# Last attention round projected in native float32, the outputs' last additions moved to VectorE, the small feed-forward group last

## The chip, the cores and the metric

The kernel runs on one core of a Trainium2 chip. The metric is the device time in microseconds of one launch, the median of several runs. A profile is one more execution, with every engine's instructions on record. Engines are named as the profile does: PE is TensorE (PEld its weight loads), DVE VectorE, ACT ScalarE, POOL GpSimd, SP SyncE; a trailing q is an engine's sequencer.

## The reference

A gated mix of two branches over one input x of 2048 tokens by 512 features:

```python
x = A_x                                    # [1, 2048, 512]
g = sigmoid((x * gate_w).sum(-1, keepdims=True))
# A: 32 heads of 16, one shared key and value head
q = (x @ wq).reshape(B, S, 32, 16).transpose(0, 2, 1, 3)
p = softmax(einsum("bhqd,bkd->bhqk", q, x @ wk) * 16 ** -0.5)
a = einsum("bhqk,bkd->bhqd", p, x @ wv).transpose(0, 2, 1, 3).reshape(B, S, 512) @ wo
# B: feed-forward, 512 -> 1792 -> 512
b = silu(x @ w1) @ w2
out = g * a + (1 - g) * b
```

All arrays are float32.

## The kernel before

Large products are made of float16 halves: each operand is split into a float16 value and a float16 rest, and three products (high by high, high by rest, rest by high) make one float32-like product. Attention's second product works otherwise: the exponentials stand in float32, and a key step of 64 keys takes either the route "A" and "B" (bfloat16 upper part, then the rest that VectorE subtracts out at L1158) or the route "N", one native float32 product, which needs no VectorE work.

Queries are cut into NCH = 4 chunks of 512 tokens, heads into NO = 4 groups of 8. That makes 16 rounds, and each round goes over 32 key steps of two half steps: 1024 score tiles (L1146) and 1024 exponentials on ScalarE (L1152, 128 by 1024 each). Into this loop the feed-forward is woven: for each chunk, F = 14 tiles of 128 in groups GF = (4, 4, 4, 2), first h (`ffn_h`, tanh on ScalarE, SiLU and a cast of the high half over a GpSimd DMA, L884), then four output products per group (`ffn_o`, one for each block of 128 tokens). When a chunk's four attention rounds are normalised, its projection by wo runs too (`out_proj`). Every output block of 128 tokens is summed in an accumulator `acc` on VectorE (`add_out`, L819 and L821), with the gate as a per-token scale, and stored when its last part is in; the last chunk has one part more, since its fourth round is projected by itself.

The order inside the loop is written by a small planner when the program is built: it keeps a clock for PE, ACT and DVE with fixed costs (PASS 0.217, WHOLE 0.866, EXP 0.905 and so on), and at each step takes the engine whose next task starts first. For PE the candidates are a score tile "S", a PV product "P", and a stream "F" of feed-forward and projection passes. A pass of the stream joins one tile that uses the array's lower 64 rows with one that uses its upper 64 rows; if there is no partner, half the array stays empty. The stream's sequence comes from `outs()`, which goes through `blocks`, the list of chunks and groups; the last chunk has an order of its own, `LAST`. VectorE's work stands in `tasks` with due times. The loop ends when at most four feed-forward outputs are left.

Behind the loop (L1418 to L1452) the stream's rest is finished, the last round is normalised (`norm_a` to `norm_b`: transposes, a sum, a reciprocal, a product, a transpose), O is split into halves (`norm_c`, L124 and L125), and the last round is projected by twelve float16 products of 128 by 512 (L844). A flag `aside` is on there: a part that is added while it is on goes over ScalarE (a scaled copy into `e`, L816) and GpSimd (an addition, L817), and its block is stored from ScalarE's queue; the last three blocks are added by VectorE and stored from SyncE's queue.

After this every engine loads a flag (L1456), jumps over a second pass that does not run for these inputs (L1457), waits for its queues, and meets the others at the end (L1482). The flag comes from `chores`, which gather maxima in the last quarter of the loop; they use `qx`, the query buffer, as scratch.

Of the kernel before, what the change touches and what calls it, by code (L numbers as in the profile page):

```python
# [21 lines left out]
NF = max(GF)  # L22
LAST = (3, 0, 1, 2)
ACCS = 4
# [24 lines left out]
def kernel(  # L49
# [62 lines left out]
    for o in range(NO):  # L112
        for c in range(NCH):
            qd[o, c] = dram.tile([128, 2, 512], F16, name=f"qd{o}_{c}")
            sh[o, c] = dram.tile([8, 2, 512], F16, name=f"sh{o}_{c}")
    md = dram.tile([128], F32, name="md")

    def split(a1, a2, a, scale):
# [95 lines left out]
    def cleared():  # L214
        for q in qb_:
            nc.gpsimd.memset(q, 0.0)
        for t_ in (VP, VF, nus):
# [478 lines left out]
    def chores():  # L696
# [13 lines left out]

        qf = qx.bitcast(F32)

        def gather():

            mt, mr, mq = qf[:, 384:416], qf[:, 416:417], qf[:, 448:480]
# [4 lines left out]
            nc.vector.transpose(mq, qf[:, 416:448])  # L720
            nc.sync.dma_start(md.rearrange("(a b) -> a b", a=4), mq[0:128:32])

        m, m1 = qf[0:1, 0:128], qf[0:1, 128:160]

        def row():
            nc.sync.dma_start(m, md.rearrange("(o p) -> o p", o=1))

        g = qf[0:1, 256:256 + 4 * len(RANGES)].rearrange("p (a b) -> p a b", a=4)

# [65 lines left out]
    def attention(ctx, scale_of, t_scale, shifts, split_pieces, chores, q_todo, bounds, early, gates_):  # L795
# [10 lines left out]

        def add_out(c, t, po, gate):
            n = c * 4 + t
            if n not in accs:
                assert n < ACCS or parts[n - ACCS] == n_parts(n - ACCS)  # L810
                accs[n] = wp.tile([128, D], F32, name="acc", bufs=ACCS)
            a = accs[n]
            if aside[0]:
                assert n in parts
                e = wp.tile([128, 512], F32, name="e", bufs=2)
                nc.scalar.activation(e, po, AF.Copy, scale=gate[:, n:n + 1])  # L816
                nc.gpsimd.tensor_tensor(a, a, e, op=OP.add)  # L817
            elif n not in parts:
                nc.vector.tensor_scalar(a, po, gate[:, n:n + 1], None, op0=OP.mult)  # L819
            else:  # L820
                nc.vector.scalar_tensor_tensor(a, po, gate[:, n:n + 1], a, op0=OP.mult, op1=OP.add)  # L821
            parts[n] = parts.get(n, 0) + 1
            if parts[n] == n_parts(n):
                (nc.scalar if aside[0] else nc.sync).dma_start(out[n * 128:n * 128 + 128], a)

# [145 lines left out]
        def bound(new, t):  # L971
# [6 lines left out]
            def shift(t):  # L978
# [5 lines left out]
                def close(t):  # L984
                    note()
                    open_q.pop()
                    if not kept:
                        e_left[0] += 1

                task(t + 9, t, 0.6, close)  # L990

            task(t, t, 0.6, shift, True)

        urgent = []
# [115 lines left out]

        def norm_c(st, key, t):
            O = wp.tile([128, 2, 512], F16, name="O", bufs=NO)
            split_v(O[:, 0], O[:, 1], st["OT"])
# [4 lines left out]

            if o == NO - 1 or c == NCH - 1 and o == NO - 2:
                all_ = {q: Os.pop((c, q)) for q in range(NO) if (c, q) in Os}  # L1120
# [196 lines left out]
        def pe_next():  # L1317
# [8 lines left out]
            if x:  # L1326
                r, s = x
                cands.append((r, 1 if n_exp[0] - 2 * s >= LAG else 3 if left_of[s][0] != "N" else 4, "P", s))
            if n_early[0]:
# [52 lines left out]
        def on_act(t, x):  # L1382
# [4 lines left out]
            exponential(p)  # L1387
            exp_done[p] = t + EXP_DONE
            n_exp[0] += 1
            decide(*divmod(p, 2))  # L1390
# [19 lines left out]
        pack_next(pack(), 0.0)  # L1410
        piece_next(0.0)
        if gates_:
            task(20.0, 0.0, 0.6, lambda t: gates_())
# [72 lines left out]
```

## Time and profile before

| | us |
|---|---|
| three runs | 1048.05, 1048.07, 1049.81 |
| median | 1048.07 |
| profiled execution | 1049.44 |
| its span, first to last instruction | 1047.6 |
| TensorE busy in the span | 1013.8 |
| ScalarE busy | 998.4 |
| VectorE busy | 940.8 |
| GpSimd busy | 60.4 |

The span is shorter than the execution's own time by what lies around the instructions. Busy times are sums over stages with different limits. A matmul's end in the profile is modelled, so TensorE's share says little of its peak.

### The profile page before, as it was taken

To read this page: it belongs to the slowest core of one execution; us is meant where nothing else is said; L and a number is where in the kernel's file an instruction comes from. 1 tells how busy PE (TensorE), PEld (TensorE's weight loads), DVE (VectorE), ACT (ScalarE), POOL (GpSimd) and SP (SyncE) were. 2 spreads that over 40 slices of the span, in tenths; PEclk is the share of its full clock that TensorE was granted. 3 is DMA by queue.
4 is the path that set the end of the run, shared out by engine and by line. 5 is a ranking of instruction groups with operands and counts; after the bars stand their busy time and mean duration, and the time that the engine had idled before them with its cause. 6 is when DMAs were issued, how large, how long until landed. Compare 5 with 4: busy or idle time off the path is not lost.

```text
span 1047.6 us, 63988 instructions
## 1 busy us (share of the span) xinstructions
PE 1013.8 (97%) x30021; PEld 555.7 (53%) x30021; DVE 940.8 (90%) x1196; ACT 998.4 (95%) x1119; POOL 60.4 (6%) x134
## 2 busy tenths in 40 slices
PE   9989999999999999999999999999999999999994
PEld 6345555555555555555555555555555555555562
DVE  6888887799999999999989999998999999999994
ACT  5899999999999999999999999999999999999991
POOL 3011111100000000000000000000000000000001
PEclk9999999999999999999999999999999999999998
DMA  6222222211011020111001021010110110101001
GB/s 215 87 64 69 80 64 69 65 44 24 5 31 37 24 45 14 35 23 21 19 14 34 34 49 19 20 29 9 40 24 9 46 33 14 34 9 19 9 4 45
DMA packets 28699, 40.18 MB, mean 38 GB/s; under 512 B 5897, under 2 KB 19978, under 8 KB 28426
## 3 DMA queue, kind: packets, MB, share of 16 engines
q0 software_dynamic: 10656, 15.73, 7.3%
q1 hardware_dynamic: 17194, 19.94, 6.1%
q8 instruction: 237, 3.88, 1.5%
q10 hardware_dynamic: 576, 0.33, 0.1%
q14 instruction: 36, 0.29, 0.1%
HBM read 20.11 MB, written 8.52 MB: 27 GB/s over the span
## 4 chain that ended last, share of the span: by engine, by line
PE 56%; ACT 28%; issue 7%; DVE 6%; DMA 1%; SPq 0%; ACTq 0%; DVEq 0%; POOLq 0%
ACT P L1152 26%; PE pm L840 22%; PE pv L1172 18%; PE S L1146 14%; DVE L L1158 2%; ACT e L871 2%; DVE raw L1158 1%; DMA xn<-in_A_x_dram 1%; PE pm L844 1%; PE pk L448 1%; DVE e L874 1%; DVE acc L821 0%; PE pt L328 0%; DVE mxs L139 0%; DMA H<-e 0%
## 5 line engine op out<-in xcount | busy, mean ns | idle before, releaser
L1152 ACT ACTIVATE P<-S 128x1024 f32<-128x1024 f32 x1024 | 959.2, 1077 | 13.5 <-PE pv L1172 7.4
L1146 PE MATMUL S<-qb,KT 50*32 50x512 f16 x8192 | 445.8, 380 | 14.7 <-ACT P L1152 11.8
L1158 DVE TENSOR_TENSOR L<-P 128x1024 f16<-128x1024 f32 x332 | 394.9, 1217 | 30.3 <-ACT P L1152 29.6
L1146 PEld LDWEIGHTS <-KT 50*32 50x32 f16 x8192 | 202.4, 89 | 265.0 <-issue 176.8
L840 PE MATMUL pm<-xs,w1s 64*32 64x512 f16 x5376 | 303.4, 375 | 2.1 <-DVE acc L821 0.9
L840 PE MATMUL pm<-w2s,H 64*32 64x512 f16 x5376 | 297.2, 375 | 0.9 <-DVE e L874 0.5
L1172 PE MATMUL pv<-P,VF 64*32 64x512 f32 x4096 | 277.1, 589 | 0.0
L1158 DVE TENSOR_TENSOR raw<-P 128x1024 f16<-128x1024 f32 x180 | 215.3, 1217 | 7.6 <-ACT P L1152 7.2
L840 PEld LDWEIGHTS <-w1s 64*32 64x32 f16 x5376 | 128.3, 92 | 54.3 <-issue 11.8
L840 PEld LDWEIGHTS <-H 64*32 64x32 f16 x5376 | 126.9, 92 | 53.1 <-issue 11.4
L1172 PE MATMUL pv<-P,VP 64*32 64x512 bf16 x2048 | 116.9, 386 | 0.0
L1172 PEld LDWEIGHTS <-VP 64*32 64x32 f16 x4096 | 74.5, 92 | 37.0 <-issue 9.9
L1172 PEld LDWEIGHTS pv<-P,VF 64*32 64x32 f32 x4096 | 80.9, 106 | 23.5 <-issue 2.9
L1172 PE MATMUL pv<-L,VP 64*32 64x512 f16 x1328 | 91.5, 376 | 0.1
L840 PE MATMUL pm<-xs,wqs 64*32 64x512 f16 x1152 | 84.8, 375 | 0.0
L884 POOL DMA_DIRECT2D H<-e x56 | 29.7, 531 | 767.0 <-DVE e L874 710.9
L840 PE MATMUL pm<-wo_s,O 64*32 64x512 f16 x1440 | 70.8, 375 | 0.1
L1172 PE MATMUL pv<-raw,VP 64*32 64x512 f16 x720 | 56.4, 376 | 0.0
L874 DVE SCALAR_TENSOR_TENSOR e<-e,pm 128x512 f32<-128x512 f32 x56 | 38.3, 684 | 11.4 <-ACT e L871 11.2
L888 DVE TENSOR_TENSOR H<-e,H 128x512 f16<-128x512 f32 x56 | 38.3, 684 | 3.5 <-DMA H<-e 3.5
L821 DVE SCALAR_TENSOR_TENSOR acc<-pm,g,acc 128x512 f32<-128x512 f32 x46 | 34.4, 749 | 7.7 <-PE pm L840 6.8
L840 PEld LDWEIGHTS <-wqs 64*32 64x32 f16 x1152 | 34.8, 92 | 11.5 <-issue 2.2
(179 smaller groups left out, 477.4 us busy)
## 6 DMA issues: line engine op xcount, KB each, us to landing
H<-e POOLq DMA_DIRECT2D x56, 128.0 KB, 2.3
qb<-qd SPq DMA_DIRECT2D x192, 32.0 KB
raw<-in_B_w_dram POOLq DMA_DIRECT2D x24, 256.0 KB, 3.1
xn<-in_A_x_dram SPq DMA_DIRECT2D x8, 512.0 KB
out_dram<-acc SPq DMA_DIRECT2D x15, 256.0 KB
qd<-qx SPq DMA_DIRECT2D x12, 256.0 KB
raw<-in_A_wo_dram POOLq DMA_DIRECT2D x4, 256.0 KB, 2.9
qb<-sh SPq DMA_DIRECT2D x60, 2.0 KB
```

What stands on the lines that cost most here:

```text
L448: nc.tensor.matmul(pk[64 * h:64 * h + 64], wkvs[:, i, kt], xs[:, j, kt, (c + h) * 512:(c + h) * 512 + 512], start=kt + n == 0, stop=kt == ...
L821: nc.vector.scalar_tensor_tensor(a, po, gate[:, n:n + 1], a, op0=OP.mult, op1=OP.add)
L840: nc.tensor.matmul(self.bank[32 * m:32 * m + 32], l(i, rows, 32 * m), r(j, rows), start=first, stop=last)
L844: nc.tensor.matmul(self.bank, l(i, slice(0, 128), 0, 128), r(j, slice(0, 128)), start=first, stop=last)
L871: nc.scalar.activation(e, o.bank, AF.Tanh, scale=t_scale)
L874: nc.vector.scalar_tensor_tensor(e, e, 1.0, o.bank, op0=OP.add, op1=OP.mult)
L884: nc.gpsimd.dma_start(H[:, 0], e)
L888: nc.vector.tensor_tensor(H[:, 1], e, H[:, 0], op=OP.subtract)
L1146: nc.tensor.matmul(sc[32 * m:32 * m + 32, f], KT[b:b + 50, k0:k0 + 32], qtile[i][b:b + 50, m // 2, j], start=True, stop=True)
L1152: nc.scalar.activation(probs[s][:, 2 * j:2 * j + 2], banks.pop(p), AF.Exp, scale=scale_of(*rounds[steps[s][0]]))
L1158: nc.vector.tensor_tensor(lows[s, j], probs[s][:, js], upper(probs[s])[:, js], op=OP.subtract)
L1172: nc.tensor.matmul(pvs[i][h][32 * j:32 * j + 32], a[r], b[r], start=k == 0 and n != "B", stop=k == NK - 1 and n != "A")
```

## The change

Five edits, all in or behind the loop of attention:

- `LAST` goes from (3, 0, 1, 2) to (0, 1, 2, 3): the group of two feed-forward tiles is the last one of the last chunk.
- The last round is not split into halves (`norm_c` returns at once). Instead the transposed O (`state["OT"]`, float32) is the stationary operand of four native float32 products with the last 128 rows of wo, which `load_last` brings as float32 into `qx` once no query block is open any more. `qx` is no longer free as scratch, so the chores use the new tile `sc` and the first row of `ident`. The gate of these products is `g2`, the gate with the scale of wo multiplied in, made once, 60 exponentials before the end.
- `add_out` loses its way over ScalarE and GpSimd: all additions are VectorE's. Behind the loop the odd blocks are stored from ScalarE's queue and the even ones from SyncE's.
- When the last exponential is planned, a PV product goes ahead of the stream (priority 1).
- Behind the loop the normalisation goes ahead of the additions that are left; then come the four products, each into a bank of its own, and their additions.

```diff
-LAST = (3, 0, 1, 2)
+LAST = (0, 1, 2, 3)
...
+    sc = consts.tile([128, 96], F32)
+    g2 = consts.tile([128, 4], F32)
...
-        def add_out(c, t, po, gate):
+        def add_out(c, t, po, gate, m=None):
             n = c * 4 + t
+            m = n if m is None else m
...
-            if aside[0]:
-                assert n in parts
-                e = wp.tile([128, 512], F32, name="e", bufs=2)
-                nc.scalar.activation(e, po, AF.Copy, scale=gate[:, n:n + 1])
-                nc.gpsimd.tensor_tensor(a, a, e, op=OP.add)
-            elif n not in parts:
-                nc.vector.tensor_scalar(a, po, gate[:, n:n + 1], None, op0=OP.mult)
+            if n not in parts:
+                nc.vector.tensor_scalar(a, po, gate[:, m:m + 1], None, op0=OP.mult)
             else:
-                nc.vector.scalar_tensor_tensor(a, po, gate[:, n:n + 1], a, op0=OP.mult, op1=OP.add)
+                nc.vector.scalar_tensor_tensor(a, po, gate[:, m:m + 1], a, op0=OP.mult, op1=OP.add)
             parts[n] = parts.get(n, 0) + 1
             if parts[n] == n_parts(n):
-                (nc.scalar if aside[0] else nc.sync).dma_start(out[n * 128:n * 128 + 128], a)
+                (nc.scalar if aside[0] and t % 2 else nc.sync).dma_start(out[n * 128:n * 128 + 128], a)
...
                     open_q.pop()
+                    if not open_q:
+                        load_last()
...
+        wl = qx.bitcast(F32)
+
+        def load_last():
+            nc.sync.dma_start(wl, wo[(NO - 1) * 128:NO * 128])
...
         def norm_c(st, key, t):
+            if key == rounds[-1]:
+                return
...
-            if o == NO - 1 or c == NCH - 1 and o == NO - 2:
+            if o == NO - 1 - (c == NCH - 1):
...
-                cands.append((r, 1 if n_exp[0] - 2 * s >= LAG else 3 if left_of[s][0] != "N" else 4, "P", s))
+                cands.append((r, 1 if n_exp[0] - 2 * s >= LAG or n_exp[0] == 2 * len(steps) else 3 if left_of[s][0] != "N" else 4, "P", s))
...
+            if p == 2 * len(steps) - 60:
+                task(t + 20, t, 0.1, lambda t: nc.vector.tensor_scalar(g2, gg[:, 4 * (NCH - 1):4 * NCH], split_pieces.so, None, op0=OP.mult))
...
-        ends, banks_ = [], halves()
+        ends, banks_ = [], halves() + halves()
         while work.next or left[0]:
             o, work.next = work.next or next(seq), None
             if o is not None:
-                o.bank = banks_.pop(0) if banks_ else bank()
+                o.bank = banks_.pop(0)
                 whole([o], range(len(o.mm)))
                 ends.append(o)
         while tasks:
-            n = min((n for n, x in enumerate(tasks) if x[1]() is not None), key=lambda n: tasks[n][0])
+            n = min((n for n, x in enumerate(tasks) if x[1]() is not None), key=lambda n: (tasks[n][4], tasks[n][0]))
             now["DVE"] += on_dve(now["DVE"], n)
-        for o in ends[:1]:
+        for o in ends:
             o.add()
-        outs_ = [o() for o in urgent]
-        for o, b in zip(outs_, [bank(), bank()] + halves()):
-            o.bank = b
-        whole(outs_, range(2))
-        whole(outs_, range(2, 3 * NO))
-        for o in ends[1:] + outs_:
-            o.add()
-            aside[0] = o in ends
-
+        banks_ += [bank() for _ in ends]
+        for t, b in enumerate(banks_):
+            nc.tensor.matmul(b, state["OT"][:, t * 128:t * 128 + 128], wl, start=True, stop=True)
+        for t, b in enumerate(banks_):
+            add_out(NCH - 1, t, b, g2, t)
```

More of the change, by code (lines that the diff above doesn't have):

```diff
@@ L216, in cleared @@
             nc.gpsimd.memset(q, 0.0)
-        for t_ in (VP, VF, nus):
+        for t_ in (VP, VF, nus, sc):
             nc.gpsimd.memset(t_, 0.0)
@@ L709, in chores @@
         todo.append(lambda: absmax(mxs[:, M_VV:M_VV + 1], VF[:, :, 1:17], AX.XY))
-        qf = qx.bitcast(F32)
         def gather():
-            mt, mr, mq = qf[:, 384:416], qf[:, 416:417], qf[:, 448:480]
+            mt, mr, mq = sc[:, 0:32], sc[:, 32:33], sc[:, 64:96]
             nc.vector.tensor_reduce(mr[0:64], um, axis=AX.X, op=OP.min)
@@ L719, in gather @@
             nc.vector.tensor_reduce(mr, mt, axis=AX.X, op=OP.max)
-            nc.vector.transpose(mq, qf[:, 416:448])
+            nc.vector.transpose(mq, sc[:, 32:64])
             nc.sync.dma_start(md.rearrange("(a b) -> a b", a=4), mq[0:128:32])
-        m, m1 = qf[0:1, 0:128], qf[0:1, 128:160]
+        m, m1 = ident[0:1], sc[0:1, 0:32]
         def row():
             nc.sync.dma_start(m, md.rearrange("(o p) -> o p", o=1))
-        g = qf[0:1, 256:256 + 4 * len(RANGES)].rearrange("p (a b) -> p a b", a=4)
+        g = ident[0:1, 0:4 * len(RANGES)].rearrange("p (a b) -> p a b", a=4)
         def check(n0):
@@ L1411, in attention @@
         piece_next(0.0)
+        if not open_q:
+            load_last()
         if gates_:
```

## The prediction

> **What bounds the kernel now.** I read the page first, then the instructions of the program's last lines (the branch at L1457 and the closing at L1482), then the chain of waits from 1000 us on, then windows and tiles of the stretch that the change rewrites.
>
> ```profile
> span 1047.6 us, 63988 instructions
> PE 1013.8 (97%) x30021; PEld 555.7 (53%) x30021; DVE 940.8 (90%) x1196; ACT 998.4 (95%) x1119; POOL 60.4 (6%) x134
> ...
> 530.00:776.00 246.00, 244.03 (x7656) 134.80 (x7635) 230.38 (x259) 243.85 (x272) 7.40 (x14) 1.00 0.12 27
> 776.00:1022.50 246.50, 240.79 (x7432) 135.59 (x7423) 229.34 (x280) 244.76 (x272) 7.93 (x15) 1.00 0.10 21
> ```
>
> The first two lines are the page's, the last two are windows (length, then busy time of PE, PEld, DVE, ACT and POOL). The second window is the last quarter of the loop, and it is the only part of the loop that the change re-plans. ScalarE is busy 244.76 of 246.50 us there. So before the last score the new order can win at most 1.74 us of ScalarE's idle time, however much TensorE saves.
>
> Behind the loop the bound is another. These are the sequencers' instructions at the end (count, minimum/median/maximum ns, first and last start in us):
>
> ```profile
> L1457 POOLq INC_SWDGE_SEM  x1: 1991/1991/1991, 1037.3 to 1037.3; - x1
> L1457 ACTq COMPARE_BRANCH  x1: 54/54/54, 1037.9 to 1037.9; - x1
> L1457 SPq COMPARE_BRANCH  x1: 45/45/45, 1038.4 to 1038.4; - x1
> L1457 SPq EVENT_SEMAPHORE  x8: 17/17/17, 1041.7 to 1042.2; - x8
> L1482 POOLq DRAIN  x3: 50/107/7414, 1039.3 to 1047.3; - x3
> L1482 SPq DRAIN  x3: 7/7/7, 1043.0 to 1047.0; - x3
> L1482 ACTq DRAIN  x2: 8/8/8, 1041.0 to 1047.0; - x2
> L1482 DVEq DRAIN  x2: 10/14/17, 1039.6 to 1047.0; - x2
> L1482 PEldq DRAIN  x2: 8/10/13, 1039.0 to 1047.1; - x2
> ```
>
> SyncE, ScalarE, VectorE and TensorE reach their first closing drain at about 1043.1, 1041.0, 1039.6 and 1039.0. GpSimd starts a drain at 1039.3 that lasts 7.41 us, to 1046.75; only then do the others go on, at 1047.0. So the last 3.65 us before the final 0.84 us belong to GpSimd alone. Its drain is late because of what stands ahead of it:
>
> ```profile
> 990.83 0.53 POOL L884 DMA_DIRECT2D H<-e  x1 [28.76 <-DVE e L874]
> 1029.53 1.28 POOL L817 TENSOR_TENSOR acc<-acc,e 128x512 f32<-128x512 f32 x1 [38.18 <-ACT e L816]
> 1032.41 1.28 POOL L817 TENSOR_TENSOR acc<-acc,e 128x512 f32<-128x512 f32 x1 [1.60 <-ACT e L816]
> 1035.61 1.26 POOL L817 TENSOR_TENSOR acc<-acc,e 128x512 f32<-128x512 f32 x1 [1.91 <-ACT e L816]
> ```
>
> The timeline of POOL: its loop work ends at 990.83, and the three additions of L817 hold it until 1036.87. The chain of waits does not show this, because it ends at the last arithmetic:
>
> ```profile
> 1002.92 0.86 PE pv L1172 x16
> ...
> 1022.64 0.22 PE S L1146 x8
> ...
> 1023.08 0.86 PE pm L840 x32
> ...
> 1026.11 0.98 PE pv L1172 x16
> 1027.09 1.31 DVE T L1089 x2
> ...
> 1031.39 0.72 DVE T L1109
> ...
> 1032.14 0.44 DVE O L124
> ...
> 1032.63 0.61 PE pm L844 x2
> ...
> 1035.00 0.76 DVE acc L821
> ...
> 1036.32 0.74 DVE acc L821
> ```
>
> **The change part by part.** Edits with one answer first. The additions of L816/L817 disappear from ScalarE and GpSimd and go to VectorE. The new load of wo's last 128 rows in float32 (256 KB) stands on SyncE's queue at about score 769 of 1024; it holds the queue as long as a store of the same size (0.36 us, SPq row below), and what is queued behind it is the exchange of the maxima and the query loads of the next round, 64 exponentials ahead of their use: nothing. Nor do the scratch tiles, the small product for the gates and one memset at the start cost anything that the end waits for.
>
> Loop. Counted in the built instruction order, the passes between score 769 and the last score are 440 feed-forward or projection passes instead of 443, with two drains of TensorE fewer, the rest alike. The row "0.86 x32" is four passes of eight, 0.215 each: 0.65 us less TensorE work, of which ScalarE's bound lets little through. I take 0.2, bounds 1.7 of gain (all of the idle time above) and 1.7 of loss (the idle time doubled).
>
> From the last score to the last PV product. Before: 1022.86 to 1027.09, 4.23 us. After, the order puts PV first and holds one half product, two passes and three native float32 products (0.86 each, row at 1002.92): 0.22 + 0.43 + 2.58 = 3.23, a gain of 1.0. Together the last PV ends at 1027.09 - 1.2 = 1025.9.
>
> Normalisation is unchanged: 1027.09 to 1032.11 is 5.02 us, so the transposed O is there at 1030.9. The two halves of O (L124/L125, 0.5 us ahead of the first product) fall away.
>
> Projection. Four native products of 128 columns by 512 take the place of twelve float16 ones. Nearest row: 0.86 us for one native pass of the whole array, so 3.46. The price could be more by exposed weight loads, but the products are long; I take 3.46. Their signals come in pairs in the built program (after the second and the fourth product), so two additions start after each. Meanwhile VectorE does the two left-over feed-forward additions:
>
> ```profile
> L821 DVE SCALAR_TENSOR_TENSOR acc<-pm,g,acc x46: 739/750/754, 208.2 to 1024.0; 128x512 f32<-128x512 f32 x46
> L821 DVE SCALAR_TENSOR_TENSOR acc<-S,gg,acc x2: 742/742/742, 1035.7 to 1036.3; 128x512 f32<-128x512 f32 x2
> L824 SPq DMA_DIRECT2D out_dram<-acc x15: 332/356/1187, 329.4 to 1037.7; - x15
> L824 ACTq DMA_DIRECT2D out_dram<-acc x1: 363/363/363, 1036.9 to 1036.9; - x1
> ```
>
> Two at 0.75 are 1.5 us, inside the 1.73 of the first two products. If those ran late, each would move the end by up to 0.75.
>
> Clock. This is the cost that is not shown. TensorE's feed-forward rest behind the last PV was long before and is short after:
>
> ```profile
> 1026.77 4.83 PE L840 MATMUL pm<-w2s,H 64*32 64x512 f16 x112
> ...
> 1035.00:1035.50 0.50, 0.39 (x2) 0.00 (x0) 0.50 (x1) 0.50 (x1) 0.00 (x0) 1.00 0.00 0
> 1037.50:1038.00 0.50, 0.00 (x0) 0.00 (x0) 0.00 (x0) 0.00 (x0) 0.00 (x0) 0.92 0.51 160
> 1038.00:1038.50 0.50, 0.00 (x0) 0.00 (x0) 0.00 (x0) 0.00 (x0) 0.00 (x0) 0.50 1.05 369
> ```
>
> Before, TensorE worked until 1031.60 and started again at 1032.63: 1.03 us idle, and the clock stayed. After, eight passes and a drain (1.9 us) stand behind the last PV instead of twenty, so TensorE idles from 1027.8 to 1030.95, 3.15 us. The windows show what an idle time can do: the last product ended at 1035.39, and the granted clock (the 0.92) fell to half at 1037.92, 2.5 us later. A gap of 3.15 us is nearer to the 2.5 that had the fall than to the 1.03 that had none. So I let the clock fall. No row shows how long it stays low: the bounds are no extra time and 3.46 us (all four products at half clock); I take the middle, 1.6.
>
> The Trainium skill, "TensorE: Matmul & The Clock Gate", section "What's actually happening", says that the clock halves after at least one idle window of about 3.4 us, free-running, and comes back after a busy one; the trace agrees that the clock halves, but its fall came 2.5 us after the last product, within less than a full idle window. By the page's window a low stretch would cost about 1.7 us.
>
> End. The products end at 1030.95 + 3.46 + 1.6 + 0.17 (pipeline) = 1036.2; the third addition ends at 1036.9, the fourth at 1037.6. SyncE stores blocks 0 and 2, ScalarE blocks 1 and 3. From the issue of its last store SyncE needed 5.39 us to its drain before (1037.7 to 1043.1: issue, branch, 3.3 us to the first instruction behind it, checks), so it drains at 1042.35. ScalarE needed 4.1 from issue to drain (1036.9 to 1041.0): 1041.7. GpSimd's wait, INC_SWDGE_SEM and drain (0.4 + 2.0 + 7.4 = 9.9 us with gaps, from 1036.87 to 1046.75) now follow its last H cast. In the built order that stands 36 VectorE instructions ahead of the end, 16 of them of this kind:
>
> ```profile
> L1158 DVE TENSOR_TENSOR L<-P 128x1024 f16<-128x1024 f32 x332 | 394.9, 1217 | 30.3 <-ACT P L1152 29.6
> ```
>
> At 1.22 us for these and 0.75 for most others that is over 30 us, so the loop hides them. Without that cover they would cost up to 3.65 us again. The barrier's rest adds 0.84: 1043.2 us against 1047.6, 4.4 us less. The profiled execution took 1049.44 us, its span and 1.84 around it, 1.37 above the median of the three runs; I take the difference off the median: 1048.07 - 4.4 = 1043.7.
>
> **The rivals.**
> (B) The clock holds. The gap is 3.15 us and the only fall seen came after an idle time that never ended; for it speaks that 1.03 us did nothing. By the skill's page named above this is the likelier course, since a 3.15 us gap cannot fill a 3.4 us window. Then the 1.6 go: 1042.1.
>
> (C) GpSimd's 7.41 us drain is not its own length but waits for the others' quiet. Against it: it started before the last stores had landed and outlasted SyncE by 3.65 us, with no wait named. For it: the trace has it once only, at the very end. Then it would end as far behind the last addition as now: 1046.75 - 1037.06 = 9.7 us behind 1037.6, which is 1048.1 in the span with the 0.84; on the median 1048.6 at the low clock, and 1047.0 at the full one.
>
> (D) The re-planned last quarter starves ScalarE. With the small group last, outputs and casts fall at other places, and each exponential that waits for its scores is paid in full, since ScalarE is the bound. Price: 256 exponentials by 0.027 us each are 6.9 us. It decides from 4.4 + 2.1 = 6.5 us of added idle time on, against 1.74 now; the quarter before lost 2.15, so nothing in the trace has that size. Then 1043.7 + 6.9 = 1050.6.
>
> That the change does not do what it says I rule out: the four native products stand in the built order, and no addition on GpSimd.
>
> **How the numbers follow.** My forecast has 0.62, B 0.20, C 0.12, D 0.06. The forecast alone spans 1041.8 (a low stretch of little cost, a better loop) to 1046.0 (all products at half clock, or ScalarE losing 1.7); B spans 1040.5 to 1043.8. Forecast and B together make 0.82, so the range is 1040.8 to 1046.2. What a measurement of this kernel can tell is 0.2%, 2.1 us: faster means below 1046.0. Of the forecast 0.60 lie there, all of B, and 0.02 of C: 0.82. Within 0.2%: the rest of the forecast, most of C and a third of D: 0.13. Slower: 0.05.
>
> **What would show it.** In the profile after: POOL's long drain begins before 1025 us and SyncE's closing drain comes last; no L817; the last PV ends near 1026; four native products start 5 us behind it, with the granted clock at 0.50 over part of them; additions in pairs; the closing near 1043. I am wrong if the long drain still ends last, if the clock stays at 1.00 (then B), or if ScalarE's idle time in the last quarter has grown by microseconds.

## Result and profile after

The changed kernel takes 1041.65 us, median of six runs (1040.56 to 1042.31), against 1048.06 us of six runs of the kernel before on the same chip: a ratio of 0.9935, 95% interval 0.9923 to 0.9948, 6.4 us less. In two later groups of runs, beside 1049.97 and 1049.54 of the kernel before, its ratios were 0.9924 and 0.9922. The forecast was 1043.7 with a range of 1040.8 to 1046.2.

The page of the changed kernel begins so (this execution took 1042.31 us):

```profile
span 1040.4 us, 63976 instructions
...
PE 1011.1 (97%) x30017; PEld 558.3 (54%) x30017; DVE 937.3 (90%) x1196; ACT 994.9 (96%) x1116; POOL 56.7 (5%) x132
```

The sequencers' closing instructions, now L1487, in the changed kernel (count, minimum/median/maximum ns, first and last start in us):

```profile
L1487 POOLq DRAIN  x3: 50/107/7414, 1002.0 to 1040.2; - x3
L1487 SPq DRAIN  x3: 7/7/7, 1039.6 to 1039.9; - x3
...
L1487 ACTq DRAIN  x2: 8/8/8, 1038.7 to 1039.9; - x2
```

GpSimd's drain lasts 7414 ns as before, but starts at 1002.0 and is over at 1009.5, inside the loop. ScalarE's first closing drain comes at 1038.7, SyncE's at 1039.6 as the last, and the span ends 0.82 us behind that.

The changed kernel's timeline behind the last score (start, busy, engine, line, operation, tiles, count, and in brackets the idle time ahead of it; L817 is now VectorE's addition, L820 the stores):

```profile
1022.34 2.77 PE L1177 MATMUL pv<-P,VF 64*32 64x512 f32 x48
...
1024.92 2.23 PE L836 MATMUL pm<-w2s,H 64*32 64x512 f16 x40
...
1025.21 1.31 DVE L1092 STREAM_TRANSPOSE T<-pv 128x512 f32<-128x512 f32 x2 [4.46 <-PE pv L1177]
...
1028.24 0.69 DVE L1107 TENSOR_TENSOR U<-T,rr 128x512 f32<-128x512 f32 x1
...
1029.82 3.67 PE L1456 MATMUL S<-qx,T 128*128 128x512 f32 x8 [2.67 <-DVE T L1112]
...
1032.60 2.07 SPq L820 DMA_DIRECT2D out_dram<-acc  x2
...
1033.53 1.41 DVE L817 SCALAR_TENSOR_TENSOR acc<-S,g,acc 128x512 f32<-128x512 f32 x2 [0.31 <-PE S L1456]
```

PV products of the last round end where VectorE's first transpose starts, 1025.21; TensorE's rest is done at 1027.15; the four native products (two records each) run from 1029.82 to 1033.49, and the last addition ends at 1034.94. The next table gives the stretches of the profiled executions, from the start of exponential 768 on (the start of the last quarter); the last two columns are profiles of the same changed kernel in the two later groups.

| stretch, us | before | forecast | after | after, 2nd group | after, 3rd group |
|---|---|---|---|---|---|
| exponential 768 to end of last score | 245.63 | 245.43 | 243.81 | 244.09 | 242.37 |
| to the end of the last PV | 4.21 | 3.23 | 3.33 | 3.32 | 3.32 |
| normalisation | 5.04 | 5.02 | 4.47 | 4.46 | 4.46 |
| to the end of the last product | 3.28 | 5.23 | 3.81 | 5.52 | 5.52 |
| to the end of the last addition | 1.68 | 1.4 | 1.45 | 1.44 | 1.45 |
| to the end of the span | 10.52 | 5.6 | 5.50 | 5.33 | 4.98 |
| sum | 270.36 | 265.9 | 262.37 | 264.16 | 262.10 |

So 5.0 of 8.0 us come from the close (4.9 forecast) and 0.9 from the way to the last PV (1.0); the loop gave 1.8 and the normalisation 0.6, which I had at 0.2 and nothing. The products took 0.5 us more than before, the last addition 0.2 less. The clock, which I let fall in the gap, held there in the first profile and fell in the two others.

The pair of profiles differs by 8.0 us and the medians by 6.4: exponential 768 starts 0.84 us later in the profile after (778.07 against 777.23), and the execution profiled before was 1.38 us above its median, the one after 0.66.

### The profile page after: what moved, and what is told of

It reads as the page before. It is cut to its first block, busy times and chain, and to the rows that moved or that the text cites. A ratio compares the mean times of both kernels' runs of the same rounds, so it can differ in the third digit from the quotient of the medians.

```text
span 1040.4 us, 63976 instructions
## 1 busy us (share of the span) xinstructions
PE 1011.1 (97%) x30017; PEld 558.3 (54%) x30017; DVE 937.3 (90%) x1196; ACT 994.9 (96%) x1116; POOL 56.7 (5%) x132
## 4 chain that ended last, share of the span: by engine, by line
PE 61%; ACT 28%; DVE 5%; issue 4%; DMA 1%; SPq 0%; ACTq 0%; DVEq 0%
ACT P L1157 26%; PE pm L836 24%; PE pv L1177 20%; PE S L1151 15%; DVE L L1163 2%; ACT e L867 2%; DMA xn<-in_A_x_dram 1%; DVE raw L1163 1%; PE pm L840 1%; PE pk L450 1%; DVE acc L817 0%; DVE e L870 0%; PE pt L330 0%; PE pt L481 0%; PE S L1456 0%
## 5 line engine op out<-in xcount | busy, mean ns | idle before, releaser
L1151 PE MATMUL S<-qb,KT 50*32 50x512 f16 x8192 | 444.5, 380 | 14.5 <-ACT P L1157 11.7
L836 PE MATMUL pm<-w2s,H 64*32 64x512 f16 x5376 | 293.0, 376 | 0.5 <-DVE qx L947 0.2
L836 PEld LDWEIGHTS <-w1s 64*32 64x32 f16 x5376 | 130.9, 93 | 50.3 <-issue 9.6
L836 PE MATMUL pm<-wo_s,O 64*32 64x512 f16 x1440 | 68.1, 375 | 0.0
L817 DVE SCALAR_TENSOR_TENSOR acc<-pm,g,acc 128x512 f32<-128x512 f32 x48 | 35.8, 747 | 6.8 <-PE pm L836 6.1
```

Source lines behind the costliest of these rows:

```text
L817: nc.vector.scalar_tensor_tensor(a, po, gate[:, m:m + 1], a, op0=OP.mult, op1=OP.add)
L836: nc.tensor.matmul(self.bank[32 * m:32 * m + 32], l(i, rows, 32 * m), r(j, rows), start=first, stop=last)
L1151: nc.tensor.matmul(sc[32 * m:32 * m + 32, f], KT[b:b + 50, k0:k0 + 32], qtile[i][b:b + 50, m // 2, j], start=True, stop=True)
```

## Experiments

The theory: what pays is that GpSimd closes early; the order and the priority shorten the way to the last PV product; native float32 pays little by itself; and the granted clock falls after a 3.41 us step in which TensorE had little to do. The rivals stand in each expectation. Every kernel was timed beside the kernel before on its own chip, so ratios are compared. Line numbers in quoted rows are those of each experiment's own kernel.

**GpSimd works last again.** The changed kernel with one tiny GpSimd copy behind the last addition:

```diff
             add_out(NCH - 1, t, b, g2, t)
+        nc.gpsimd.tensor_copy(sc[:, 0:1], accs[NKT - 1][:, 0:1])
```

> The changed kernel with one GpSimd copy of 128 by 1 behind the last addition. Theory (GpSimd's closing chain has a length of its own, about 9.9 us from its last instruction to the end of its long drain, and only its place in time changed): the last addition ends near 1035, so the drain ends near 1045 and the span near 1045.8, 5.4 us more than the changed kernel's 1040.4; time near 1047, about the kernel before. Rival (the drain is long only where something else keeps GpSimd from closing, and a short instruction alone changes nothing): span near 1040.5, time near 1041.7.

1048.92 us, ratio 0.9994 [0.9985, 1.0003]: all of the gain is gone. Its timeline of POOL behind the last addition:

```profile
1034.52 0.19 POOL L1459 COPY sc<-acc 128x1 f32<-128x1 f32 x1 [38.67 <-DVE acc L817]
```
Its closing instructions of GpSimd:

```profile
L1488 POOLq DRAIN  x3: 50/107/7414, 1038.4 to 1046.3; - x3
```

A copy of 0.19 us moves the long drain to 1038.4, and the span ends at 1046.63, 12.25 us behind the last addition instead of 5.50. That is 6.75 us in the profile for an instruction whose result nobody reads. The drain keeps its length of 7414 ns. Together with the profile after, where it was over at 1009.5 while the other engines were at work, this refutes rival C of the prediction: the drain does not wait for the others' quiet, and it costs what stands behind their close.

**Only GpSimd is relieved.** The kernel before, with all its additions on VectorE and the normalisation ahead of them:

```diff
-            if aside[0]:
-                ...
-                nc.gpsimd.tensor_tensor(a, a, e, op=OP.add)
-            elif n not in parts:
+            if n not in parts:
...
-            n = min(..., key=lambda n: tasks[n][0])
+            n = min(..., key=lambda n: (tasks[n][4], tasks[n][0]))
```

> The kernel before with one part of the change: the additions behind the loop are all VectorE's (two left-over ones placed behind the normalisation); order of groups and float16 halves as before. Theory: GpSimd's drain is hidden, and the normalisation's product loses the 0.6 us by which it was longer beside a GpSimd addition; VectorE gets 2.2 us more additions. Last addition near 1037.2, SyncE's closing near 1042.6, span near 1043.4 against 1047.6, time near 1043.9: two thirds of the whole gain. Rival (the gain is the new order's and the native projection's): time within 1 us of the kernel before, 1047 to 1049.

1048.62 us, ratio 0.9988 [0.9979, 0.9997]: 1.0 us won instead of the 4.2 expected. The drain is hidden here too (it starts at 995.2), and the span ends 5.81 us behind the last addition instead of 10.52, but the timeline shows where the gain was given back:

```profile
1030.03 0.69 DVE L1099 TENSOR_TENSOR U<-T,rr 128x512 f32<-128x512 f32 x1
...
1031.96 0.69 DVE L125 TENSOR_TENSOR O<-T,O 128x512 f16<-128x512 f32 x1
...
1032.57 1.40 DVE L816 SCALAR_TENSOR_TENSOR acc<-pm,g,acc 128x512 f32<-128x512 f32 x2
1033.37 0.38 PE L839 MATMUL pm<-wo_s,O 128*128 128x512 f16 x1 [1.84 <-DVE acc L816]
```

The first float16 product waits 1.84 us (TensorE's idle time in brackets) for VectorE's two additions out of the `pm` banks, which now stand behind the halves of O; then the clock is at half from 1035.01 to 1038.42, and the twelve products take 4.59 us instead of 2.76. The last addition comes 12.43 us behind the last PV product instead of 10.00. Taking the additions from GpSimd pays only if they do not stand between the normalised O and its banks; in the changed kernel the first native product waits for nothing but VectorE's transpose (the bracket of its row above).

**Old order of the groups.** The changed kernel with `LAST = (3, 0, 1, 2)`:

```diff
-LAST = (0, 1, 2, 3)
+LAST = (3, 0, 1, 2)
```

> The changed kernel with the old order of groups in the last chunk (3, 0, 1, 2). Theory: the loop's last quarter is as before; behind the last PV product stand 15 stream passes and 12 whole products, 6 us of TensorE work, more than the 4.5 us of the normalisation, so the native products start 1.4 us later against it, while the last PV comes 0.6 us earlier behind the last score; no idle gap, so the clock holds. Time 0.7 to 1.5 us above the changed kernel, near 1042.7. Rival (the place of the small group does nothing): 1041.65, the changed kernel's own.

1046.48 us, ratio 0.9966 [0.9952, 0.9979], 3.2 to 4.6 us above the changed kernel by its three ratios, where I expected about 1. Its timeline:

```profile
1026.19 3.75 PE L836 MATMUL pm<-w2s,H 64*32 64x512 f16 x72
...
1029.87 2.76 PE L840 MATMUL S<-w2s,H 128*128 128x512 f16 x12
...
1033.48 2.84 PE L1456 MATMUL S<-qx,T 128*128 128x512 f32 x6 [0.85 <-DVE acc L817]
```

The last PV product ends at 1026.48. Around and behind it stand 72 records of feed-forward passes and 12 whole products of the big group that is now last, where the changed kernel has 40 and none. TensorE works on them until 1032.63, 1.7 us longer than VectorE needs for O, and then stands still for 0.85 us because an addition has to free a bank. The first native product so starts 7.0 us behind the last PV instead of 4.61. I had counted the passes and not the bank. I had also left out the loop: from exponential 768 to the last score this kernel takes 245.66 us, as the kernel before does (245.63), against 242.37 to 244.09 of the changed kernel's three profiles. So 1.6 to 3.3 us of the loss lie in the loop, and it is the order of the groups that shortens the loop.

**No priority for the last PV products.**

```diff
-... or n_exp[0] == 2 * len(steps) else 3 ...
+... else 3 ...
```

> The changed kernel without the priority of PV products when the last exponential is planned. All stream passes then stand ahead of the last PV: it ends 1.7 us later, and TensorE idles for the whole normalisation, near 4.5 us. Theory (the clock falls in such a gap and the native products pay): granted clock 0.5 over part of the four products, which take 4.5 to 6.9 us instead of 3.7; time 2.9 to 4 us above the changed kernel, 1044.5 to 1045.7. Rival (the clock does not fall or does not come back into it): products 3.7 us, time 1.7 us above, near 1043.3.

1044.30 us, ratio 0.9946 [0.9932, 0.9959], 1.2 to 2.5 us above the changed kernel by its three ratios. This is less than the 2.9 to 4 us of the theory; the changed kernel that it is compared with pays for a fall in many runs too. The profile decides for the theory. The last PV product ends 5.40 us behind the last score instead of 3.33, which is 2.07 us; the passes are then done ahead of it, and TensorE stands still while VectorE normalises. The windows (length, busy time of PE, PEld, DVE, ACT and POOL with counts, then granted clock) around it:

```profile
1026.91:1030.32 3.41, 0.00 (x0) 0.00 (x0) 3.27 (x7) 0.00 (x0) 0.00 (x0) 1.00 0.00 0
1030.32:1033.73 3.41, 3.04 (x4) 1.52 (x5) 0.22 (x1) 0.00 (x0) 0.00 (x0) 0.50 0.02 5
```
And the native products in its timeline:

```profile
1030.69 5.18 PE L1456 MATMUL S<-qx,T 128*128 128x512 f32 x8 [4.71 <-DVE T L1112]
```

A step of 3.41 us with nothing on TensorE is followed by one at half clock, and the four products take 5.18 us.

**The changed kernel again**, unaltered, in the two later groups:

> The changed kernel unaltered, for its times and its profile beside the three kernels that follow. On the first chip its ratio to the kernel before was 0.9935. Theory (the granted clock may fall at any 3.41 us step in which TensorE's array was used little, wherever the phase of these steps lies): ratio 0.9925 to 0.9945, and in the profile either a fall behind the gap (four native products 5.2 us) or one inside the loop, or none. Rival (the clock fell inside the loop because of where the plan puts the work there): the fall lies again near 956 us.

> The changed kernel unaltered, on the same chip. Ratio 0.9920 to 0.9940; mean clocks between 0.995 and 0.999. Where its profile has 0.995, two falls are in it (one inside the loop near 956 us, one behind the gap); with 0.999 none.

1042.28 us, ratio 0.9924 [0.9911, 0.9938], and 1041.56 us, ratio 0.9922 [0.9908, 0.9935]. Here are windows of the first profile after, cut at the clock's own steps:

```profile
952.78:956.20 3.42, 2.07 (x63) 0.72 (x55) 3.42 (x4) 3.42 (x5) 0.19 (x1) 1.00 0.27 43
956.20:959.61 3.41, 3.41 (x56) 1.40 (x55) 3.36 (x4) 2.45 (x3) 0.00 (x0) 0.50 0.00 0
1027.88:1031.29 3.41, 1.47 (x4) 0.78 (x5) 3.02 (x6) 0.00 (x0) 0.00 (x0) 1.00 0.00 0
1031.29:1034.70 3.41, 2.20 (x6) 0.66 (x4) 2.58 (x4) 0.00 (x0) 0.00 (x0) 1.00 0.38 142
```
The same of the second group's profile:

```profile
952.49:955.90 3.41, 2.06 (x64) 0.64 (x52) 3.41 (x4) 3.41 (x5) 0.27 (x1) 1.00 0.28 43
955.90:959.32 3.42, 3.42 (x56) 1.38 (x63) 3.31 (x4) 2.39 (x3) 0.00 (x0) 0.50 0.00 0
1027.59:1031.00 3.41, 1.41 (x4) 0.73 (x5) 3.08 (x6) 0.00 (x0) 0.00 (x0) 1.00 0.00 0
1031.00:1034.41 3.41, 3.41 (x6) 1.25 (x4) 1.41 (x2) 0.00 (x0) 0.00 (x0) 0.50 0.28 91
```
And the second profile's products in its timeline:

```profile
1029.59 5.37 PE L1456 MATMUL S<-qx,T 128*128 128x512 f32 x8 [2.66 <-DVE T L1112]
```

In both, a step in the loop with 2.07 or 2.06 us of work on TensorE is followed by one at 0.50. In the gap the first has 1.47 us of work in its step and keeps 1.00; the second, whose steps lie 0.06 us earlier against the products, has 1.41 and gets 0.50 next: its products take 5.37 us instead of 3.67, 1.70 more. Falls and rises of one execution lie on a grid: 956.20 and the last fall at 1038.12 are 24 steps of 3.413 us apart, 955.90 and 1031.00 are 22. The third profile's steps lie otherwise again: its step from 953.06 had 2.84 us of work and no fall came, the one from 1024.74 had 1.12 and its products took 5.37 too. So in these profiles it is the place of the grid that decides whether the changed kernel pays. The fall near 956 us came again in the second profile, as the rival says, and not in the third: the plan leaves TensorE little to do there, and the grid decides how much of it one step holds. In the profile of the longer gap (below) that step had 2.08 us of work, 0.01 more than in the first profile, and no fall came:

```profile
952.80:956.22 3.42, 2.08 (x56) 0.91 (x63) 3.42 (x4) 3.42 (x5) 0.00 (x0) 1.00 0.27 43
956.22:959.63 3.41, 3.41 (x121) 1.95 (x112) 3.41 (x5) 3.41 (x5) 0.00 (x0) 1.00 0.00 0
```

**The last round in halves.** The changed kernel with float16 halves of the last O and twelve products in the same four S banks:

```diff
-            nc.tensor.matmul(b, state["OT"][...], wl, start=True, stop=True)
+            for i, j in ((0, 0), (0, 1), (1, 0)):
+                nc.tensor.matmul(b, state["O"][:, i, ...], wo_s[:, j, NO - 1], ...)
```

> The changed kernel with its last round split into float16 halves and projected in twelve float16 products out of the same four S banks. Theory (the native float32 product buys little by itself, what paid was GpSimd's close and the order): VectorE makes two halves, 0.9 to 1.1 us, before the left-over additions; the twelve products take 2.6 to 2.8 us against 3.67 of the four, the last addition comes 0.2 to 0.5 us later behind the last PV than the 9.73 us of the changed kernel, the time is 0 to 0.6 us above it: ratio to the kernel before 0.9935 to 0.9945. Rival (the native product is what pays): 1.5 us or more above the changed kernel, ratio over 0.9950.

1041.90 us, ratio 0.9920 [0.9906, 0.9933], beside 0.9924 of the changed kernel on the same chip: no difference that these runs can tell, and the rival is out. Its timeline:

```profile
1029.43 0.69 DVE L127 TENSOR_TENSOR O<-T,O 128x512 f16<-128x512 f32 x1
...
1029.46 5.30 PE L1458 MATMUL S<-wo_s,O 128*128 128x512 f16 x12 [3.04 <-DVE O L126]
```

The halves delay the first product by 0.37 us only (4.98 behind the last PV instead of 4.61), since the products begin after the first half. In this profile two steps ran at half clock, so the twelve products took 5.30 us and nothing can be read from that figure.

**Work in the gap.** The changed kernel with ten products that nobody reads, ahead of the native ones:

```diff
+        full = pO.tile([128, 512], F32, name="pv0")
+        for _ in range(10):
+            nc.tensor.matmul(full, w2s[:, 0, 0, 0:128], w2s[:, 0, 0], start=True, stop=True)
         for t, b in enumerate(banks_):
```

> The changed kernel with ten float16 128x512 products, whose result nobody reads, on TensorE between the last PV product and the native products, while VectorE normalises. Theory (the clock falls behind a 3.41 us step with little use of the array): the granted clock stays at 1.0 through the four native products in the profile, they take 3.5 to 3.7 us, and the median is 0 to 0.9 us below the changed kernel (0.5 times the 1.7 us that a fall costs): ratio 0.9925 to 0.9935. Rival (the fall is set by something else than the use of the array): the fall is as frequent as without them, ratio as the changed kernel's, or up to 0.5 us above it for the ten products in front.

1040.72 us, ratio 0.9913 [0.9899, 0.9926]; 1.56 us below the changed kernel on the same chip, more than I expected of the gap alone. Its timeline:

```profile
1024.73 2.33 PE L1457 MATMUL pv<-w2s 128*128 128x512 f16 x10
...
1027.38 3.70 PE L1459 MATMUL S<-qx,T 128*128 128x512 f32 x8 [0.32 <-DVE T L1112]
```

The ten take 2.33 us out of the idle time, the native products start 0.05 us behind O, and the clock stays at 1.00 from 5.88 us to 1033.29, behind the last product.

**A longer gap.** One more VectorE pass over O, in place:

```diff
+        nc.vector.tensor_scalar(state["OT"], state["OT"], 1.0, None, op0=OP.mult)
         for t, b in enumerate(banks_):
```

> The changed kernel with one more VectorE pass over the normalised output (times 1.0, in place) behind the left-over additions and ahead of the native products: the gap without work on TensorE grows by 0.5 to 2.0 us to over 3.41 us. Theory: the granted clock falls behind the gap more often than in the changed kernel; where it falls the four products take 5.2 to 5.4 us; the time is 1.9 us above the changed kernel without a fall and 3.3 to 3.6 us with it, ratio 0.9953 to 0.9970. Rival (no clock term at all): only the added delay of 0.5 to 2.0 us, products 3.7 us, ratio 0.9940 to 0.9955.

1044.49 us, ratio 0.9946 [0.9932, 0.9960], 2.2 us above the changed kernel on the same chip. The products in its timeline:

```profile
1029.65 6.19 PE L1457 MATMUL S<-qx,T 128*128 128x512 f32 x8 [4.29 <-DVE T L1455]
```
Its windows from the gap on:

```profile
1024.49:1027.90 3.41, 0.87 (x19) 0.22 (x8) 3.27 (x8) 0.00 (x0) 0.00 (x0) 1.00 0.00 0
1027.90:1031.31 3.41, 1.66 (x2) 0.84 (x3) 1.61 (x3) 0.00 (x0) 0.00 (x0) 0.50 0.03 5
1031.31:1034.72 3.41, 3.41 (x5) 1.35 (x4) 1.28 (x2) 0.00 (x0) 0.00 (x0) 0.50 0.04 5
```

The products start 1.62 us later and take 6.19 us, 2.52 more than in the first profile after: the step with 0.87 us of work brings half clock, and the next, with 1.66 us of work at half clock, keeps it for one step more. By its ratio alone this falls in the rival's interval; the profile decides for the theory. My size was too big because the changed kernel that it is compared with pays for a fall in many runs too.

**One queue for the last stores**, on top of the filled gap:

```diff
-                (nc.scalar if aside[0] and t % 2 else nc.sync).dma_start(...)
+                (nc.scalar if aside[0] else nc.sync).dma_start(...)
```

> The changed kernel with the ten products that fill the gap, and with all four last stores issued from ScalarE's queue (the changed kernel alternates SyncE and ScalarE). In the changed kernel's trace ScalarE's closing drain came at 1038.7 and SyncE's at 1039.6, though SyncE's last store was issued 0.67 us before ScalarE's. Theory (SyncE's 5.31 us from its last store to its drain is what ends last): SyncE closes early, ScalarE's drain ends the program 3.7 us behind its last issue, end of the span 14.0 to 14.5 us behind the last PV product instead of 15.0, the time 0.5 to 1.0 us below the kernel with filled gap alone: ratio to the kernel before 0.9903 to 0.9912. Rival (what takes the time is the last store's landing, whichever queue issues it): no gain, or a loss of up to 0.7 us as four issues stand on one queue: 0.9910 to 0.9920.

1040.16 us, ratio 0.9910 [0.9895, 0.9925], not to be told from 0.9913, and inside both intervals; the span ends 15.44 us behind the last PV product instead of 15.01, where the theory has 14.0 to 14.5. The profile decides for the rival. SyncE's branch and its semaphores behind it in this kernel:

```profile
L1465 SPq COMPARE_BRANCH  x1: 45/45/45, 907.6 to 907.6; - x1
L1465 SPq EVENT_SEMAPHORE  x8: 17/17/17, 1036.6 to 1037.1; - x8
```
Its stores, in the timeline:

```profile
1030.72 2.71 ACTq L820 DMA_DIRECT2D out_dram<-acc  x4
```

SyncE has no store of its own any more, yet its first semaphore comes through at 1036.6 only, 3.2 us behind the end of the last issue (1033.44), and its checks then go one after another to its drain at 1038.0. The branch lies 129 us back, so it is not what holds SyncE. The DMA records show what does: the last packet of the stores ends at 1036.16, and behind it (1036.17 to the end) the DMA queues have instructions alone (queue, packets, MB, share):

```profile
q14 instruction: 2, 0.02, 1.1%
```

SyncE's first semaphore follows that packet by 0.44 us. In all twelve profiles of the changed kernel and its variants it follows the last packet of the four stores, whichever queue issued them, by 0.37 to 0.47 us (by 1.29 in the profile before and 0.16 in that with only GpSimd relieved, where SyncE issued the last store). So the last store's landing ends last, 2.72 us behind the end of its issue here.

**Halves with the filled gap and one queue:** the two edits above together with the halves.

> The same with the last round in float16 halves again: twelve float16 products in place of the four native ones, ten products in the gap in front of them, all last stores on ScalarE's queue. Theory (with the clock held, the twelve take 2.6 to 2.8 us and the halves hold the first up by 0.4 us: the native products cost 0.5 us against them): last addition 9.0 to 9.4 us behind the last PV product instead of 9.66, time 0.3 to 0.7 us below the kernel with four native products and the same queue: ratio 0.9897 to 0.9908. Rival (native is the faster form): 0.3 us or more above that kernel.

1041.24 us, ratio 0.9922 [0.9908, 0.9935], 1.08 us above the kernel with native products beside it: the theory missed, and the number is the rival's, though the two intervals overlap. Its timeline:

```profile
1028.59 0.69 DVE L127 TENSOR_TENSOR O<-T,O 128x512 f16<-128x512 f32 x1
...
1028.61 3.06 PE L1461 MATMUL S<-wo_s,O 128*128 128x512 f16 x12 [0.78 <-DVE O L126]
1029.20 1.40 DVE L817 SCALAR_TENSOR_TENSOR acc<-pm,g,acc 128x512 f32<-128x512 f32 x2
...
1030.52 2.72 DVE L817 SCALAR_TENSOR_TENSOR acc<-S,gg,acc 128x512 f32<-128x512 f32 x4
```

With the clock held the twelve products take 3.06 us instead of 3.70, but VectorE has become the bound: the second half, two left-over additions and four final ones follow each other without a pause from 1028.59 to 1033.24, so the last addition comes 9.61 us behind the last PV instead of 9.67. The 0.64 us won on TensorE buys nothing, since VectorE has the halves to make; the last addition does not tell the two forms apart. The span's end lies 0.83 us further behind the last PV than in the kernel beside it, and so does the last packet of the stores, at 1037.20: 13.57 us behind the last PV against 12.76. The last issue ends no later (9.98 against 10.04), so it is the landing that took longer; why it did stays open.

**Work in the loop as well.** The kernel with the filled gap, and score products 949 to 956 issued twice:

```diff
-            for m in range(4):
+            for m in 2 * (0, 1, 2, 3) if 949 <= p < 957 else range(4):
```

> The changed kernel with the gap filled by ten products, and with the score products of eight exponentials (949 to 956 of 1024) issued twice into the same banks, 0.22 us more each, at the place where the changed kernel's profile had TensorE idle for 0.5 us at a time and then 3.41 us of half clock. Theory (the clock falls behind a 3.41 us step in which TensorE had too little to do, so what is given to it there holds the clock): no half clock between 20 us and the last product, a mean clock of 0.999 in nearly every run (the changed kernel's runs had 0.995 to 0.999, and those with the gap filled 0.997 to 0.999), the loop from exponential 768 to the last score 242.2 to 242.8 us as in the profiles without a fall, and the median 0.3 to 0.9 us below the kernel with the gap filled alone: ratio 0.9900 to 0.9912. Rival (the fall inside the loop comes from something else): clock means spread as before, ratio 0.9912 or more for the added products.

1041.04 us, ratio 0.9917 [0.9903, 0.9930], 0.5 us below the changed kernel beside it, and not better than the filled gap alone, where the theory expected 0.3 to 0.9 us less; by its ratio it falls to the rival. The step of its own grid where the products were added:

```profile
952.05:955.46 3.41, 3.10 (x112) 1.52 (x96) 3.41 (x4) 3.41 (x5) 0.53 (x1) 1.00 0.26 43
```

No fall comes, and the stretch from exponential 768 to the last score is 242.67 us, as in profiles without a fall (242.30 with the filled gap). The mean clocks of the runs were 0.998 to 0.999. That the added products were needed is not shown: in the three profiles with the gap filled and without them, the emptiest step there had 2.41, 2.24 and 2.33 us of work, and no fall came either. Over all runs: of sixteen of the changed kernel eight had a mean clock of 0.996 or less; of nineteen with the gap filled (four kernels) none had. The mean also counts the half clock behind the last product, so it tells falls only in the sum. The profiles tell them apart: with the new order and the gap left open the clock fell behind the gap in six of seven, with the gap filled in none of four.

## Why the prediction was right, point by point

- **Close.** GpSimd's long drain began before 1025, SyncE closed last, 5.31 us behind its last issue (5.39 forecast), and the span ended 0.82 us later (0.84). The copy at the end shows that the drain has a length of its own and that the gain needs it out of the way; the kernel before without GpSimd's additions shows that this is not enough. That SyncE's 5.31 us met the forecast was luck: I counted them from SyncE's own store, but SyncE's checks follow the landing of the last store (above), and in the changed kernel ScalarE's queue issues that one. In the two later profiles the same distance was 5.14 and 4.80 us.
- **From the last score to the last PV:** 3.33 against 3.23. Without the priority it is 5.40.
- **Loop: the step that was mis-sized.** I gave the new order 0.2 us, and at most 1.74, because ScalarE was "busy" 244.76 of 246.50 us. Measured, the quarter is 1.5 to 1.8 us shorter in the two profiles with a fall in it and 3.3 in the third. The gain is the new order's, since with the old one the changed kernel's quarter is as long as before (245.66). What was wrong is the bound: ScalarE's records overlap. This group is ScalarE's exponentials from 962 to 1024 us before (count, busy us and mean ns of one, idle time):

```profile
L1152 ACT ACTIVATE P<-S 128x1024 f32<-128x1024 f32 x65 | 61.1, 1041 | 0.8 <-PE S L1146 0.3
```
The same after:

```profile
L1157 ACT ACTIVATE P<-S 128x1024 f32<-128x1024 f32 x66 | 61.1, 1084 | 0.1
```

One exponential's record lasts 1.04 to 1.08 us, yet they follow each other faster than that, as ScalarE's timeline of before shows (start, time of the group, count):

```profile
970.61 18.07 ACT L1152 ACTIVATE P<-S 128x1024 f32<-128x1024 f32 x19 [0.29 <-PE S L1146]
...
989.05 35.00 ACT L1152 ACTIVATE P<-S 128x1024 f32<-128x1024 f32 x37
```
And that of after:

```profile
963.69 32.37 ACT L1157 ACTIVATE P<-S 128x1024 f32<-128x1024 f32 x35
...
996.38 26.85 ACT L1157 ACTIVATE P<-S 128x1024 f32<-128x1024 f32 x29
```

Before, 18.07/19 and 35.00/37 are 0.951 and 0.946 us each; after, 32.37/35 and 26.85/29 are 0.925 and 0.926. Waits shorter than the overlap do not show as idle time. The last 64 exponentials took 61.24 us before and 59.55 after, 1.7 us less, of which the two group rows show 0.7 as idle time (0.8 before, 0.1 after). The rest of the quarter's gain lies ahead of them.
- **Normalisation: a term that I had at nothing.** It took 4.47 us instead of 5.04 because GpSimd's additions are gone. On VectorE's timeline of before the product U and the second half of O run beside them:

```profile
1030.09 1.27 DVE L1104 TENSOR_TENSOR U<-T,rr 128x512 f32<-128x512 f32 x1
...
1032.60 1.64 DVE L125 TENSOR_TENSOR O<-T,O 128x512 f16<-128x512 f32 x1
```

GpSimd's additions (rows in the prediction) held 1029.53 to 1030.81 and 1032.41 to 1033.69. U, begun at 1030.09, took 1.27 us instead of 0.69, and the half of O, begun at 1032.60, 1.64 instead of 0.69: both ended 0.55 us behind GpSimd's addition. With GpSimd silent both take 0.69 us (the kernel before with only GpSimd relieved, above). The Trainium skill, "SBUF — State Buffer", section "SBUF: two separate sides", says that a VectorE operation with two inputs in SBUF and a GpSimd operation that reads SBUF exclude each other from a shared pair of ports, the first holding it for its whole length; the two pairs of rows agree with it. I had taken the slow durations for the price.
- **Products and clock.** Four native products take 3.67 us at full clock (3.46 and 0.17 forecast) and 5.37 with a fall (1.70 more; 1.6 forecast). The forecast's case, a fall in the gap, happened in two of three profiles, case B in one. The gap was 2.67 us, not 3.15, and the clock fell behind it all the same, so B's argument that such a gap is too short does not hold here. The size was right; that it is a matter of chance from run to run, and that a second fall waits in the loop (956 us), was not in the prediction.
- **Rivals.** C is refuted by the copy and by the drain that ended inside the loop, D by the shorter quarter. B's figure of 1042.1 lies nearest to the median, but not for B's reason alone: in the two profiles with a fall in the gap the sums of the table are 264.16 and 262.10 against a forecast of 265.9, so loop and normalisation carried it. The forecast's own 1043.7 was 2.05 us too high for the same reason.
- **Native float32** was part of the sum as twelve products against four. Halves in its place changed the time by nothing that can be told (0.9920 and 0.9924).

The versions with the filled gap are the fastest that were run (0.9910 to 0.9917 with native products; the changed kernel 0.9922 to 0.9935). Their intervals overlap with the changed kernel's, so what is shown is the clock that holds, and of the time only the direction.

## What to carry to other kernels

Read the end of a program from the sequencers' closing instructions: one late GpSimd instruction of 0.19 us cost 6.75 us here, and work taken off it pays only when its new place holds no bank that the last products need. Judge whether an engine is saturated by the pitch of its instructions (0.95 against 0.925 us), not by its busy share, where records overlap. Where TensorE waits a few microseconds ahead of its last products, try products that nobody reads: ten of them kept its clock here in four profiles of four, at no cost that was seen. Behind GpSimd, what closed this program was the landing of its last store.

## What was not expected of the hardware

- The granted clock fell after steps in which TensorE was far from idle: 2.07 us of 3.41 in the loop (products on part of the array, 64 by 32 tiles), 1.41 us in the gap, while 2.08 us in the loop and 1.47 us in the gap did not bring it down. The Trainium skill, "TensorE: Matmul & The Clock Gate", section "What's actually happening", has one idle window of about 3.4 us and a window that runs freely: the grid of 3.413 us agrees, the idle window does not. What is counted in a step stays open: busy time alone does not order the cases (2.07 fell, 1.47 stayed), use of the array may.
- GpSimd's closing drain took 7414 ns in every profile, whether the other engines were at work or done.
- SyncE's first check behind the branch came 0.37 to 0.47 us behind the last packet of the stores in the twelve profiles of the changed kernel and its variants, even where SyncE had issued none of them.
- A float32 product of VectorE with two inputs in SBUF took 1.27 us beside a GpSimd addition and 0.69 us without.
